# Moving the end of an FFT convolution between engines: residuals, layer statistics and weight splitting off the vector engine

## The chip, the cores and the metric

The kernel runs on one core of a Trainium2 chip. The core has a matrix engine (TensorE, PE), a vector engine (VectorE, DVE), an activation engine (ScalarE, ACT), a general engine (GpSimd, POOL) and a queue engine that mostly issues DMAs (SyncE, SP). Each runs its own instructions in order; they wait for one another by semaphores. PE writes its results to PSUM, from which DVE and ACT read them; everything else lies in SBUF. The metric is the time of one execution on the device in microseconds (us), smaller is better.

## The reference, cut to what matters

Four layers stand behind one another over a stream x of 2048 tokens by 640 features, each on the layer-normalized stream and each added to it:

```python
x = A_u
x = x + conv(layernorm(x))      # "a"
x = x + attention(layernorm(x)) # "b"
x = x + conv(layernorm(x))      # "c"
x = x + attention(layernorm(x)) # "d"

def conv(u):       # a state-space kernel K, 2048 taps for each feature
    y = irfft(rfft(u, 4096) * rfft(K, 4096))[:2048]
    return y + u * Dskip
def attention(x):  # 32 query heads of 20, one shared key and value head
    q, k, v = x @ wq, x @ wk, x @ wv
    return softmax(q k^T / sqrt(20)) v @ wo
```

Both convolutions have the same parameters, and so have both attentions. `layernorm` takes mean and variance over the 640 features of a token.

## The kernel before, in words

The stream stays in SBUF as `self.x`, [128 partitions, 16, 640]: 16 rows of 128 tokens, here called tokens tau = 0 to 15.

**A convolution** (`conv_layer`, line 664) goes over five chunks of 128 features (`NCH` = 5, `DC` = 128). For one chunk: ACT normalizes the 16 token rows (line 686); PE multiplies them with a table of cosines and sines (`dense`, line 570; `raw`, line 541, for the first chunk) and ACT copies the results out; DVE does the butterflies of a radix-8 transform (`fft8` with sign -1, fourteen calls, lines 95 and 98), the complex product with the spectrum of the kernel (`product`, eight calls, line 704) and the inverse butterflies (`fft8` with sign +1); PE multiplies by the inverse table (`inverse`, line 723), in four groups g of four token rows; and `residual` (line 730) adds a group to x on DVE. The spectrum A has 16 slots: token row tau needs slots 2t and 2t+1 with t = tau mod 8. The butterflies leave t = 0 and 4 first, then 2 and 6, and the odd t from the four scalar_tensor_tensor calls at the end. A group is tau = 4g to 4g+3, so the first group already needs odd t.

The order of PE, ACT and DVE is written out by hand (`manual_schedule`, line 671). `weave(calls, between)` puts other work between the calls of a list: (5, f) means that f is issued ahead of call 5. The residuals ("turns") of chunk c stand between the forward butterflies of chunk c+1 (turns 0 and 1) and its product (turns 2 and 3); turns 0 and 1 also issue the inverse of groups 2 and 3. Results of `inverse` alternate between two PSUM banks (`ps1`), so that groups 2 and 3 need the banks of 0 and 1 back.

In the last two chunks `residual` also takes statistics for the next layer normalization on DVE (`stats_part`): BATCH_NORM_STATS2 of a token row's first 512 features behind chunk 3 (line 600), of the last 128 behind chunk 4 (line 602), then their union (line 603). `norm_part(g)` turns them into scale and shift for a group (lines 624 to 631, with one square root on ACT). The loop over the last chunk's turns and `norm_part` (line 780) stands outside the hand-written order; there a planner with costs of its own orders the instructions of all engines. The same holds for the beginning of the attention.

**The attention's weights** are split in two parts whose sum is the fp32 value: `wh`, rounded to the matmul's format by ACT (line 795), and the rest `wl`, by DVE (line 798). `attn_weights` (line 800) loads them in six pieces (keys and values, then five of 128 rows of `wq`), one staging buffer `wst` for all, and the pieces are woven into the last chunk's product. This is done in both convolutions.

**The attention's beginning** (`_attn`, line 840): `prepare(nb)` normalizes four token rows on ACT (line 872), PE transposes them (line 881), ACT and DVE split them; `project` multiplies (line 898). The main loop behind it has the exponentials on ACT (line 1028) and products on PE (lines 1024 and 1038). `add` (line 1081) adds the attention's output to x.

Of the kernel before, what the change touches and what calls it, by code (L numbers as in the profile page):

```python
# [11 lines left out]
F32 = mybir.dt.float32  # L12
# [3 lines left out]
AF = mybir.ActivationFunctionType  # L16
# [14 lines left out]
EPS = 1e-5  # L31
SCALE = 20.0**-0.5
# [52 lines left out]
def fft8(nc, A, B, R, sg):  # L85

    ADD, SUB = ALU.add, ALU.subtract  # L90
    plus, minus = (ADD, SUB) if sg < 0 else (SUB, ADD)
    calls = []

    def tt(*a):
        calls.append(lambda: nc.vector.tensor_tensor(*a))  # L95

    def stt(*a):
        calls.append(lambda: nc.vector.scalar_tensor_tensor(*a, op0=ALU.mult, op1=ADD))
# [24 lines left out]
    return calls  # L123
# [12 lines left out]
class Net:  # L136
    def __init__(self, tc, ins):
        self.tc = tc
        self.nc = tc.nc
        self.ins = ins  # L140
        self.wfs = []
        self.sts = {}
        self.bank = 0

    def setup(self, ctx):
        tc, nc = self.tc, self.nc
        self.cp = ctx.enter_context(tc.tile_pool(name="cp", bufs=1))
        self.dr = ctx.enter_context(tc.tile_pool(name="dr", bufs=1, space=DRAM))
        self.ident = self.cp.tile([P, P], F32, name="ident")
        self.halfpi = self.cp.tile([P, 1], F32, name="halfpi")  # L150
        nc.vector.memset(self.halfpi, 0.5 * math.pi)
        self.xp = ctx.enter_context(tc.tile_pool(name="xp", bufs=1))
        self.x = self.xp.tile([P, 16, D], F32, name="x")
        self.mv = self.xp.tile([P, 16, 2], F32, name="mv")
        self.kd = self.dr.tile([NCH, P, 16 * DC], F32, name="kd")
        self.kh = self.dr.tile([NCH, P, 32 * DC], F32, name="kh")
# [438 lines left out]
    def stats_part(self, t, last):  # L595

        nc = self.nc
        if not last:
            self.sts[t] = self.xp.tile([P, 2, 6], F32, tag=f"st{t}", bufs=1, name=f"sp{t}")
            nc.vector.bn_stats(self.sts[t][:, 0], self.x[:, t, 0 : D - DC])  # L600
        else:
            nc.vector.bn_stats(self.sts[t][:, 1], self.x[:, t, D - DC : D])
            nc.vector.bn_aggr(self.mv[:, t], self.sts.pop(t).rearrange("p a b -> p (a b)"))
# [5 lines left out]
    def norm_part(self, g):  # L609
        ts = slice(4 * g, 4 * g + 4)  # L610
        self.rstd(self.xp, self.mv[:, ts], self.rs[:, ts], self.nmr[:, ts], 4)
# [7 lines left out]
    def rstd(self, pool, mv, out, nmr, n):  # L619

        nc = self.nc
        ve = pool.tile([P, n], F32, tag="ve", bufs=2, name="ve")
        sq = pool.tile([P, n], F32, tag="sq", bufs=2, name="sq")
        nc.vector.tensor_scalar(ve, mv[:, :, 1], EPS, None, ALU.add)
        nc.scalar.activation(sq, ve, AF.Sqrt)
        nc.vector.reciprocal(out, sq)
        nc.vector.tensor_tensor(sq, out, out, ALU.mult)
        nc.vector.tensor_tensor(sq, sq, ve, ALU.mult)
        nc.vector.tensor_scalar(sq, sq, -0.5, 1.5, ALU.mult, ALU.add)
        nc.vector.tensor_tensor(out, out, sq, ALU.mult)  # L630
        nc.vector.scalar_tensor_tensor(nmr, mv[:, :, 0], -1.0, out, op0=ALU.mult, op1=ALU.mult)
# [32 lines left out]
    def conv_layer(self, nm, first):  # L664
# [6 lines left out]
        with tc.manual_schedule(engines={mybir.EngineType.PE, mybir.EngineType.Activation,  # L671
# [41 lines left out]

            def inverse(c, g, A):
                y = self.ps1(f"y{nm}{c}{g}")
                v = A.rearrange("p s (k d) -> p s k d", k=2)
                for s in range(4):
                    tau = 4 * g + s
                    t, j = tau % 8, tau // 8
                    i = 0  # L720
                    for kk in range(2):
                        for c_ in range(2):
                            nc.tensor.matmul(y[:, s * DC : (s + 1) * DC], self.wi[:, t, j, c_, kk],  # L723
                                             v[:, 2 * t + c_, kk], start=(i == 0), stop=(i == 3))
                            i += 1
                return y

            def residual(c, g, y):
                xs = self.x[:, 4 * g : 4 * g + 4, c * DC : (c + 1) * DC]
                tt(xs, y.rearrange("p (t d) -> p t d", t=4), xs, ALU.add)  # L730
# [19 lines left out]
            pieces = []  # L750
            late = []
            for c in range(NCH):
                A = As.pop(c)
                mul = product(A, khs.pop(c)) + fft8(nc, A, B, R, +1)
                if c == NCH - 1:
                    late += zip((0, 1, 3, 5, 7, 11), pieces)
# [20 lines left out]
                if c + 2 == NCH - 1:  # L777
                    self.wfs.pop().close()
                    pieces = self.attn_weights()
# [6 lines left out]
    def attn_setup(self):  # L786
# [3 lines left out]
        self.mxd = dr.tile([33, 2, L], F32, name="mxd")  # L790

# [8 lines left out]
    def attn_weights(self):  # L800
# [6 lines left out]
        wl = wp.tile([P, 5, 692], F32R, name="wl")  # L807
        kv = wp.tile([P, 5, 52], F32, name="kv")
# [3 lines left out]
        self.wqs = stack, wh, wl  # L812

        def piece(k):
            wst = wp.tile([P, D], F32, tag="wst", bufs=1, name=f"wst{k}")
            nc.sync.dma_start(wst, ins["B_wq"][P * k : P * k + P])
            self.split(wh[:, k, 0:D], wl[:, k, 0:D], wst, act=True)

        return [lambda: self.split(wh[:, :, D:692], wl[:, :, D:692], kv, act=True)] + [
            lambda k=k: piece(k) for k in range(5)]  # L820
# [19 lines left out]
    def _attn(self, ctx, nm, out):  # L840
# [17 lines left out]
        with tc.tile_pool(name=f"pj{nm}", bufs=1, reuse_waits="tile") as pj:  # L858
# [7 lines left out]
            def prepare(nb):  # L866

                xs = []
                for i in range(4):
                    t = 4 * nb + i  # L870
                    x = pj.tile([P, D], F32, tag="x", bufs=4, name=f"x{nb}{i}")
                    nc.scalar.activation(x, self.x[:, t], AF.Identity, scale=self.rs[:, t : t + 1],
# [114 lines left out]
    def main_loop(self, ap, mp, kt, vt, nm, out):  # L987
# [93 lines left out]
        def add(nb, u, py, last):  # L1081

            i, half = u // 2, u % 2
            t = 4 * nb + i
# [142 lines left out]
```

## Time and profile before

| | |
|---|---|
| time, median of 3 runs | 3106.16 us (3105.56 to 3109.65) |
| span of the profiled execution, first to last instruction | 3104.8 us |
| busy in the span: PE, DVE, ACT | 2851.3, 1431.9, 2391.6 us |
| mean granted clock of PE | 0.977 |
| last two chunks of convolution "a" | about 567 to 683 us |
| last two chunks of convolution "c" | about 1909 to 2024 us |

The profile is that of one execution. The page of the profile says nothing of that execution's time but the span, which is 1.36 us below the median of the runs. In the timeline a row is a group of like instructions: start, length from the first start to the last end, engine, line, operation, output<-inputs with shapes, and count; in brackets stand the idle time of the engine before it and what ended it. A row that starts ahead of the end of the row before overlaps with it in the engine's pipeline; the distance of two starts is what an instruction costs its engine. In the windows a row is a stretch of time: its length, busy time with number of instructions, the granted clock of PE, and the share and rate of the DMA.

### The profile page before, as it was taken

To read this page: it belongs to the slowest core of one execution; us is meant where nothing else is said; L and a number is where in the kernel's file an instruction comes from. 1 tells how busy PE (TensorE), PEld (TensorE's weight loads), DVE (VectorE), ACT (ScalarE), POOL (GpSimd) and SP (SyncE) were. 2 spreads that over 40 slices of the span, in tenths; PEclk is the share of its full clock that TensorE was granted. 3 is DMA by queue.
4 is the path that set the end of the run, shared out by engine and by line. 5 is a ranking of instruction groups with operands and counts; after the bars stand their busy time and mean duration, and the time that the engine had idled before them with its cause. 6 is when DMAs were issued, how large, how long until landed. Compare 5 with 4: busy or idle time off the path is not lost. (4 is left out here: it accounts for less than half of the span.)

```text
span 3104.8 us, 52109 instructions
## 1 busy us (share of the span) xinstructions
PE 2851.3 (92%) x21638; PEld 1352.4 (44%) x21638; DVE 1431.9 (46%) x1853; ACT 2391.6 (77%) x2773; POOL 35.6 (1%) x102
## 2 busy tenths in 40 slices
PE   2888998949899999999999889498999999999999
PEld 0555888847323333323233489464223323233333
DVE  7888799973122232332222399931222222222223
ACT  5777343224799999999999633055999999999997
POOL 0000000000000000000000000000000000000000
PEclk9999999979899999999999999799999999999999
DMA  6011451114310000100100210132000100100100
GB/s 142 18 28 27 165 217 55 33 30 131 115 26 23 24 25 21 27 25 21 27 24 23 111 55 28 26 109 90 22 26 22 42 24 21 44 24 21 44 18 22
DMA packets 73630, 153.45 MB, mean 49 GB/s; under 512 B 22836, under 2 KB 28980, under 8 KB 69764
## 3 DMA queue, kind: packets, MB, share of 16 engines
q1 hardware_dynamic: 67336, 132.36, 14.5%
q0 software_dynamic: 4080, 16.67, 1.4%
q8 instruction: 174, 2.85, 0.4%
q10 hardware_dynamic: 1968, 0.98, 0.1%
q14 instruction: 72, 0.59, 0.1%
HBM read 93.42 MB, written 44.50 MB: 44 GB/s over the span
## 5 line engine op out<-in xcount | busy, mean ns | idle before, releaser
L1028 ACT ACTIVATE pt<-scb 128x1024 f32<-128x1024 f32 x1024 | 942.2, 1117 | 7.6 <-PE scb L1024 6.2
L1028 ACT ACTIVATE pt<-scd 128x1024 f32<-128x1024 f32 x1024 | 942.1, 1118 | 5.1 <-DMA qpd<-mxd 3.0
L1038 PE MATMUL pob<-pt,vt 128*32 128x512 f32 x4096 | 546.6, 606 | 4.5 <-DVE on L1055 3.5
L1038 PE MATMUL pod<-pt,vt 128*32 128x512 f32 x4096 | 546.4, 605 | 4.5 <-DVE on L1055 2.5
L1024 PE MATMUL scb<-qpb,kt 62*128 62x512 f32 x2048 | 385.5, 451 | 7.2 <-DVEq L977 6.9
L1024 PE MATMUL scd<-qpd,kt 62*128 62x512 f32 x2048 | 385.5, 451 | 4.8 <-DVEq L977 4.6
L1024 PEld LDWEIGHTS scb<-qpb,kt 62*128 62x128 f32 x2048 | 166.1, 185 | 402.7 <-ACT pt L1028 392.2
L1024 PEld LDWEIGHTS scd<-qpd,kt 62*128 62x128 f32 x2048 | 166.0, 185 | 400.4 <-ACT pt L1028 392.1
L1086 DVE TENSOR_TENSOR x<-pyd,x 128x320 f32<-128x320 f32 x146 | 71.8, 492 | 560.6 <-PE pyd L1098 560.6
L1086 DVE TENSOR_TENSOR x<-pyb,x 128x320 f32<-128x320 f32 x146 | 71.8, 492 | 547.4 <-PE pyb L1098 547.4
L1058 DVE RECIPROCAL rc<-rc 128x512 f32<-128x512 f32 x62 | 207.9, 3353 | 2.1
L1038 PEld LDWEIGHTS pob<-pt,vt 128*32 128x32 f32 x4096 | 80.7, 108 | 177.7 <-issue 159.6
L1038 PEld LDWEIGHTS pod<-pt,vt 128*32 128x32 f32 x4096 | 80.6, 108 | 177.6 <-issue 159.5
L415 PE MATMUL pk<-s,m 128*64 128x32 f32 x1280 | 130.7, 295 | 13.3 <-DVE s L406 13.3
L415 PE MATMUL pk<-c,e1r 128*64 128x32 f32 x1280 | 132.1, 297 | 11.4 <-DVE c L405 11.2
L415 PEld LDWEIGHTS pk<-c,e1r 128*64 128x64 f32 x1280 | 105.2, 221 | 79.6 <-issue 52.2
L723 PE MATMUL ya<-Aa,wi 128*128 128x128 f32 x640 | 78.6, 287 | 49.8 <-DVE Aa L95 46.7
L723 PE MATMUL yc<-Ac,wi 128*128 128x128 f32 x640 | 78.5, 286 | 46.8 <-DVE Ac L95 43.7
L570 PE MATMUL za<-xna,wf 128*128 128x256 f32 x512 | 113.2, 383 | 2.7 <-ACT xna L686 2.7
L415 PEld LDWEIGHTS pk<-s,m 128*64 128x64 f32 x1280 | 108.1, 226 | 15.9 <-DVE s L406 15.9
L570 PE MATMUL zc<-xnc,wf 128*128 128x256 f32 x512 | 111.5, 379 | 2.7 <-ACT xnc L686 2.7
L572 ACT ACTIVATE Aa<-za 128x1024 f32<-128x1024 f32 x16 | 16.4, 1024 | 118.4 <-PE za L570 116.8
(278 smaller groups left out, 3168.8 us busy)
## 6 DMA issues: line engine op xcount, KB each, us to landing
kh<-kh SPq DMA_DIRECT2D x10, 2048.0 KB
kh<-kn SPq DMA_DIRECT2D x5, 2048.0 KB
qhd<-qh SPq DMA_DIRECT2D x40, 256.0 KB
qld<-ql SPq DMA_DIRECT2D x40, 256.0 KB
qpb<-qhd SPq DMA_DIRECT2D x256, 40.0 KB
qpd<-qhd SPq DMA_DIRECT2D x256, 40.0 KB
ot<-on SPq DMA_DIRECT2D x216, 40.0 KB
wf<-in_c_wf POOLq DMA_DIRECT2D x16, 512.0 KB, 8.4
```

Of the source, the lines that this page charges most:

```text
L415: nc.tensor.matmul(PK[u][64 * par : 64 * par + 64, 32 * d : 32 * d + 32], e[u][:, d, par], c[u][:, d, par], start=first, stop=not first)
L570: nc.tensor.matmul(zv[:, :, c, kk], self.wf[:, t + 4 * h, j, c, kk], x, start=(n == 0), stop=(n == 3))
L572: nc.scalar.activation(A.rearrange("p (o s) d -> p o s d", o=2)[:, :, 2 * t : 2 * t + 2], z.rearrange("p (c o e) -> p o c e", c=2, o=2), A ...
L723: nc.tensor.matmul(y[:, s * DC : (s + 1) * DC], self.wi[:, t, j, c_, kk], v[:, 2 * t + c_, kk], start=(i == 0), stop=(i == 3))
L1024: nc.tensor.matmul(sc[:, 512 * par : 512 * par + 512], kt[rows, 128 * t : 128 * t + 128], qps[nb, hg, pr][rows], start=True, stop=True)
L1028: nc.scalar.activation(pt, sc, AF.Exp, scale=SCALE)
L1038: nc.tensor.matmul(po[32 * j : 32 * j + 32], vt[:, t], pts[step, j // 2][:, 512 * (j % 2) : 512 * (j % 2) + 512], start=(t == 0), stop=(t ...
L1058: nc.vector.reciprocal(rc, rc)
L1086: nc.vector.tensor_tensor(xh, py, xh, ALU.add)
```

## The change

It touches the two convolutions' last two chunks, and renames the order of token rows everywhere.

- **Order of token rows.** Groups become the rows `TAUS`: group 0 has tau 0, 4, 8, 12, group 1 has 2, 6, 10, 14, group 2 and 3 the odd ones. The attention goes over the rows in the same order.
- **Order of the butterflies.** In `fft8` the calls for t = 0 and 4 are calls 4 and 5, for t = 2 and 6 calls 8 and 9.
- **Stream on PE.** For chunks 3 and 4 `inverse` first multiplies the identity with x into the PSUM bank, and the transform is accumulated on it. `residual` for chunk 3 is then a copy to x on ACT; for chunk 4 it is part of the statistics.
- **Statistics on ACT.** `stats_first(g)`: for four token rows the sum over 512 features (a copy with `accum_out`), the negative mean, and the sum of squares about it. `stats_last(g, y)`: for the last 128 features a copy from PSUM to x with its sum, and the squares about the same shift. Two DVE instructions for all 16 rows (`stats_base`) and eleven small ones a group (`norm_part`) join them.
- **Weights.** The low part is taken on PE: identity times the weights minus identity times the high part, in PSUM, copied out by ACT. This is done in convolution "a" only, which stores both parts to DRAM (`whd`, `wld`, 1.77 MB each); convolution "c" loads them.
- The pieces of weights, `stats_first` and `stats_base` are woven into the last chunk's calls by a list.

```diff
+NA = D - DC
+FIRST = (0, 2, 1, 3)
+TAUS = [s + 4 * n for s in FIRST for n in range(4)]
...
     tt(B[:, 4:8], A[:, 0:4], A[:, 4:8], SUB)
-    tt(R[:, 0:2], A[:, 10:15:4], A[:, 11:16:4], ADD)
-    if sg < 0:
-        tt(R[:, 2:4], A[:, 11:16:4], A[:, 10:15:4], SUB)
-        tt(B[:, 12:16:3], R[:, 0:3:2], R[:, 3:0:-2], ADD)
-        tt(B[:, 14:12:-1], R[:, 0:3:2], R[:, 3:0:-2], SUB)
-    else:
-        tt(R[:, 2:4], A[:, 10:15:4], A[:, 11:16:4], SUB)
-        tt(B[:, 12:16:3], R[:, 2::-2], R[:, 1:4:2], SUB)
-        tt(B[:, 14:12:-1], R[:, 2::-2], R[:, 1:4:2], ADD)
     tt(B[:, 8:12:3], A[:, 8:10], A[:, 13:11:-1], plus)
     tt(B[:, 10:8:-1], A[:, 8:10], A[:, 13:11:-1], minus)
     tt(A[:, 0:2], B[:, 0:2], B[:, 2:4], ADD)
     tt(A[:, 8:10], B[:, 0:2], B[:, 2:4], SUB)
+    tt(R[:, 0:2], A[:, 10:15:4], A[:, 11:16:4], ADD)
+    if sg < 0:
+        tt(R[:, 2:4], A[:, 11:16:4], A[:, 10:15:4], SUB)
+    else:
+        tt(R[:, 2:4], A[:, 10:15:4], A[:, 11:16:4], SUB)
     tt(A[:, 4:14:9], B[:, 4:6], B[:, 7:5:-1], plus)
     tt(A[:, 12:4:-7], B[:, 4:6], B[:, 7:5:-1], minus)
+    if sg < 0:
+        tt(B[:, 12:16:3], R[:, 0:3:2], R[:, 3:0:-2], ADD)
+        tt(B[:, 14:12:-1], R[:, 0:3:2], R[:, 3:0:-2], SUB)
+    else:
+        tt(B[:, 12:16:3], R[:, 2::-2], R[:, 1:4:2], SUB)
+        tt(B[:, 14:12:-1], R[:, 2::-2], R[:, 1:4:2], ADD)
...
+    def stats_first(self, g, dump):
+        nc, sm = self.nc, self.sm
+        ps = range(4 * g, 4 * g + 4)
+        for p in ps:
+            nc.scalar.activation(dump(p), self.x[:, TAUS[p], 0:NA], AF.Copy, accum_out=sm["sum"][:, p : p + 1])
+        gs = slice(4 * g, 4 * g + 4)
+        nc.scalar.activation(sm["shift"][:, gs], sm["sum"][:, gs], AF.Copy, scale=-1.0 / NA)
+        for p in ps:
+            nc.scalar.activation(dump(p), self.x[:, TAUS[p], 0:NA], AF.Square, bias=sm["shift"][:, p : p + 1],
+                                 accum_out=sm["sq"][:, p : p + 1])
+    def stats_base(self):
+        nc, sm = self.nc, self.sm
+        nc.vector.tensor_scalar(sm["base"], sm["sq"], 1.0 / D, EPS, ALU.mult, ALU.add)
+        nc.vector.tensor_scalar(sm["part"], sm["shift"], DC / D, None, ALU.mult)
+    def stats_last(self, g, y, dump):
+        nc, sm = self.nc, self.sm
+        for n in range(4):
+            p = 4 * g + n
+            nc.scalar.activation(self.x[:, TAUS[p], NA:D], y[:, DC * n : DC * n + DC], AF.Copy,
+                                 accum_out=sm["sumb"][:, p : p + 1])
+        for n in range(4):
+            p = 4 * g + n
+            nc.scalar.activation(dump(n)[:, 0:DC], y[:, DC * n : DC * n + DC], AF.Square,
+                                 bias=sm["shift"][:, p : p + 1], accum_out=sm["sqb"][:, p : p + 1])
...
             def inverse(c, g, A):
+                whole = c >= NCH - 2
+                if whole:
+                    nc.tensor.matmul(y, self.ident, stream(c, g), start=True, stop=False)
...
             def residual(c, g, y):
-                xs = self.x[:, 4 * g : 4 * g + 4, c * DC : (c + 1) * DC]
-                tt(xs, y.rearrange("p (t d) -> p t d", t=4), xs, ALU.add)
-                for tau in range(4 * g, 4 * g + 4):
-                    if c >= NCH - 2:
-                        self.stats_part(tau, c == NCH - 1)
+                if c < NCH - 2:
+                    tt(stream(c, g), y.rearrange("p (t d) -> p t d", t=4), stream(c, g), ALU.add)
+                elif c == NCH - 2:
+                    nc.scalar.activation(stream(c, g), y.rearrange("p (t d) -> p t d", t=4), AF.Copy)
+                else:
+                    self.stats_last(g, y, dump)
...
                 if c == NCH - 1:
-                    late += zip((0, 1, 3, 5, 7, 11), pieces)
+                    first_, second = self.attn_weights(scr, nm == "a")
+                    late = ([(0, late[0][1]), (0, first_[0]), (1, late[1][1]), (1, first_[1])]
+                            + [(1, lambda g=g: self.stats_first(g, dump)) for g in (0,)]
+                            + [(2, second[0]), (2, first_[2]), (2, lambda: self.stats_first(1, dump)),
+                               (3, second[1]), (3, first_[3]), (3, lambda: self.stats_first(2, dump)),
+                               (4, second[2]), (4, first_[4]), (4, lambda: self.stats_first(3, dump)),
+                               (5, second[3]), (5, first_[5]), (6, second[4]), (6, second[5]),
+                               (12, self.stats_base)])
                 weave(mul, late)
...
+        if not fresh:
+            for w, dst in parts:
+                nc.sync.dma_start(w, dst.rearrange("p (k n) -> p k n", k=5))
+            return [lambda: None] * 6, [lambda: None] * 6
...
+        def first(k):
...
+            nc.scalar.activation(hi, src, AF.Copy)
+            for o, a, _ in cuts:
+                nc.tensor.matmul(o, self.ident, a, start=True, stop=False)
+            for o, _, b in cuts:
+                nc.tensor.matmul(o, self.minus, b.bitcast(F32), start=False, stop=True)
+        def second(k):
...
+            nc.scalar.activation(ends(k)[1], src, AF.Copy)
+            if k == 5:
+                for w, dst in parts:
+                    nc.sync.dma_start(dst.rearrange("p (k n) -> p k n", k=5), w)
```

More of the change, by code (lines that the diff above doesn't have):

```diff
@@ L151, in setup @@
         nc.vector.memset(self.halfpi, 0.5 * math.pi)
+        self.minus = self.cp.tile([P, P], F32, name="minus")
         self.xp = ctx.enter_context(tc.tile_pool(name="xp", bufs=1))
@@ L154, in setup @@
         self.mv = self.xp.tile([P, 16, 2], F32, name="mv")
+        self.sm = {n: self.xp.tile([P, 16], F32, name=f"sm{n}")
+                   for n in ("sum", "shift", "sq", "sumb", "sqb", "base", "part")}
         self.kd = self.dr.tile([NCH, P, 16 * DC], F32, name="kd")
@@ L624, in rstd @@
         nc.vector.tensor_scalar(ve, mv[:, :, 1], EPS, None, ALU.add)
[L625 to L630, printed above, removed]
+        self.root(ve, sq, out)
         nc.vector.scalar_tensor_tensor(nmr, mv[:, :, 0], -1.0, out, op0=ALU.mult, op1=ALU.mult)
@@ L723, in inverse @@
                             nc.tensor.matmul(y[:, s * DC : (s + 1) * DC], self.wi[:, t, j, c_, kk],
-                                             v[:, 2 * t + c_, kk], start=(i == 0), stop=(i == 3))
+                                             v[:, 2 * t + c_, kk], start=(i == 0 and not whole),
+                                             stop=(i == 3 and (s == 3 or not whole)))
                             i += 1
@@ L790, in attn_setup @@
         self.mxd = dr.tile([33, 2, L], F32, name="mxd")
+        self.whd = dr.tile([P, 5 * 692], F32, name="whd")
+        self.wld = dr.tile([P, 5 * 692], F32, name="wld")
+        self.nc.scalar.activation(self.minus, self.ident, AF.Copy, scale=-1.0)
     def split(self, hi, lo, src, act=False):
@@ L1083, in add @@
             i, half = u // 2, u % 2
-            t = 4 * nb + i
+            t = TAUS[4 * nb + i]
             xh = self.x[:, t, 320 * half : 320 * half + 320]
```

67 lines of the change are left out of this document (44 added, 23 removed).

## The prediction, made before the result

> **What bounds the kernel now.** The span of the profiled execution is 3104.8 us; the three timed runs have a median of 3106.16, 1.36 more. The page gives no other time of that execution, so I take savings from the span and subtract them from the median.
>
> I first read the timeline of VectorE (DVE) over the end of the first convolution. Columns: start, length of the group, engine, line, operation, count, and in brackets the idle time before it.
>
> ```profile
> 579.18 2.29 DVE L704 TENSOR_TENSOR B<-Aa,kh 128x2048 f32<-128x2048 f32 x1
> ...
> 581.39 0.68 DVE L730 TENSOR_TENSOR x<-ya,x 128x512 f32<-128x512 f32 x1
> 581.99 2.28 DVE L704 TENSOR_TENSOR R<-Aa,kh 128x2048 f32<-128x2048 f32 x1
> ...
> 598.36 2.36 DVE L95 TENSOR_TENSOR B<-Aa 128x1024 f32<-128x1024 f32 x2
> 600.64 1.29 DVE L95 TENSOR_TENSOR R<-Aa 128x512 f32<-128x512 f32 x2
> ...
> 609.19 2.35 DVE L95 TENSOR_TENSOR B<-Aa 128x1024 f32<-128x1024 f32 x2
> ...
> 613.39 0.68 DVE L730 TENSOR_TENSOR x<-ya,x 128x512 f32<-128x512 f32 x1
> 614.11 2.47 DVE L600 BATCH_NORM_STATS2 sp<-x 128x6 f32<-128x512 f32 x4
> 616.50 0.67 DVE L95 TENSOR_TENSOR B<-R 128x512 f32<-128x512 f32 x1
> ...
> 626.20 0.42 DVE L798 TENSOR_TENSOR wl<-kv,wh 128x260 fp32r<-128x260 f32 x1
> 626.54 2.29 DVE L704 TENSOR_TENSOR B<-Aa,kh 128x2048 f32<-128x2048 f32 x1
> ...
> 631.85 0.81 DVE L798 TENSOR_TENSOR wl<-wst,wh 128x640 fp32r<-128x640 f32 x1
> 632.58 2.28 DVE L704 TENSOR_TENSOR R<-Aa,kh 128x2048 f32<-128x2048 f32 x1
> ...
> 662.68 2.49 DVE L98 SCALAR_TENSOR_TENSOR Aa<-B 128x512 f32<-128x512 f32 x4
> 668.59 0.69 DVE L730 TENSOR_TENSOR x<-ya,x 128x512 f32<-128x512 f32 x1 [3.42 <-PE ya L723]
> ```
>
> No row has idle time until 668.59, so DVE sets the pace up to the last butterfly, which ends at 665.17. Then TensorE (PE), by its timeline:
>
> ```profile
> 579.87 27.79 PE L570 MATMUL za<-xna,wf 128*128 128x256 f32 x128
> 607.49 10.88 PE L723 MATMUL ya<-Aa,wi 128*128 128x128 f32 x96
> 620.83 3.84 PE L723 MATMUL ya<-Aa,wi 128*128 128x128 f32 x32 [2.46 <-DVE x L730]
> 661.11 2.05 PE L723 MATMUL ya<-Aa,wi 128*128 128x128 f32 x8 [36.43 <-DVE Aa L95]
> 663.51 15.76 PE L723 MATMUL ya<-Aa,wi 128*128 128x128 f32 x120 [0.36 <-DVE Aa L98]
> 680.28 0.55 PE L881 MATMUL ptb<-ident,x 128*128 128x128 f32 x3 [1.01 <-ACT x L872]
> ```
>
> PE waits 36.43 us for DVE, then its last inverse transforms end at 679.27, 14.1 us behind the butterfly, and the attention's first tokens wait for that end. The second convolution has the same rows 1341.6 us later (its butterfly group starts at 2004.41, and 2010.18 stands for 668.59); I give its times less 1341.6.
>
> ```profile
> 2004.41 2.48 DVE L98 SCALAR_TENSOR_TENSOR Ac<-B 128x512 f32<-128x512 f32 x4
> 2010.18 0.69 DVE L730 TENSOR_TENSOR x<-yc,x 128x512 f32<-128x512 f32 x1 [3.28 <-PE yc L723]
> ```
>
> So the path is DVE to 665.17, PE to 679.27, then ScalarE (ACT) at line 872.
>
> **What leaves DVE.** In the last stretch four residuals of the chunk before the last, with their statistics, take 616.50 - 613.39 = 3.11 us each, 12.4 in all. Five low parts of the weights take 632.58 - 631.85 = 0.73 each, with the small one of keys and values (626.54 - 626.20 = 0.34) 4.0. Together 16.4 us. Without them: forward butterflies from 609.19 in 609.19 - 598.36 = 10.83; product 598.36 - 579.18 less two residuals of 0.6 (581.39 to 581.99), 18.0, ends at 638.0; four calls of the inverse butterflies (2.28 and two of 0.6), 3.5. At **641.5** DVE reaches call 12, where the change puts stats_base. The reordered butterflies cost the same: the stall in the pair at 600.64 (1.32 from start to start where two calls take 1.20) goes, and one like it comes before the first scalar_tensor_tensor, whose input is then written just ahead.
>
> **What comes to ACT.** stats_base needs the squares of all sixteen tokens, and these are 32 passes of 512 elements on ACT. Rows for their price, from the timeline of ACT:
>
> ```profile
> 681.76 0.19 ACT L625 ACTIVATE sq<-ve 128x4 f32<-128x4 f32 x1
> 681.86 0.90 ACT L872 ACTIVATE x<-x,nmrna,rsna 128x640 f32<-128x640 f32 x1
> ...
> 705.28 0.59 ACT L911 ACTIVATE qs<-pqb 128x512 fp32r<-128x512 f32 x1
> ...
> 469.39 0.87 ACT L686 ACTIVATE xna<-x,nmra,rsa 128x128 f32<-128x128 f32 x2
> 470.16 0.48 ACT L686 ACTIVATE xna<-x,nmrma,rsma 128x128 f32<-128x128 f32 x1
> ```
>
> A pass of 512 lasts 0.59; neighbours overlap by about 0.1 (0.19 long, next start 0.10 later), so 0.50 from start to start. 128 elements with a scale and a bias from memory: 0.77 for two, 0.385 each; from 512 to 128 without operands I estimate 0.20, so about 0.09 an operand. A Square with a bias takes 0.59. What no row shows is the sum along the row (accum_out). I treat it as one more small instruction for each pass: between nothing (it rides along; below that it can't go, since a second output shortens no pass) and 0.19 (the small row's whole length). I take that row's pitch, **0.10**, because ACT's neighbours overlap in every row here. A group of four tokens: 4 x 0.60 + 4 x 0.69 + 0.3 for the shift and two waits on it = 5.5; four groups 21.8.
>
> They can't start early. In ACT's order they stand behind the fourth residual copy, and that needs all of PE's inverse transforms of the chunk: 10.88 / 3 = 3.63 a group, plus the added identity product (512 columns in two instructions; the 256-column row gives 27.79 / 128 = 0.217, doubled 0.43, 0.87 in all; no row has this shape, and the bounds 0.43 and 1.3 would move each convolution by up to 7 x 0.43 = 3). 607.49 + 4 x 4.5 = 625.5, copy and hand-over 0.6: 626.1. In the second convolution stats_first ends at 626.1 + 21.8 + 0.2 = **648.1**: DVE waits 6.6 us at call 12 and passes the wait on, for every later call is queued behind. In the first, ACT also has four high parts (640 wide, 0.63) and three low parts between (two of 0.63, one of 0.3), less one high part that follows: 4.1 more, **652.2**.
>
> **The new tail.** After stats_base (two calls, 0.3) two butterfly calls (1.2) release group 0: 1.65 with the hand-over, where PE formerly waited for nearly all. PE's old tail took 679.27 - 661.11 - 0.36 = 17.8; three identity products not hidden add 2.6. Second convolution: 648.1 + 1.65 + 20.4 = 670.2, **9.1 earlier** than 679.27. In the first, PE must before that take the minus-product of the last weights (their high part leaves ACT at 652.2 + 1.4): 640 columns, then the identity, 2.0 at full clock. Is the clock full? Windows of PE, with the granted clock behind the busy time:
>
> ```profile
> 626.50:627.00 0.50, 0.00 (x0) 1.00 0.00 0
> 627.00:627.50 0.50, 0.00 (x0) 0.50 0.00 0
> ...
> 667.00:668.00 1.00, 1.00 (x7) 0.52 0.12 37
> 668.00:669.00 1.00, 1.00 (x11) 1.00 0.00 0
> ...
> 468.00:469.00 1.00, 0.43 (x3) 1.00 1.01 426
> ...
> 472.00:473.00 1.00, 0.00 (x0) 1.00 0.00 0
> 473.00:474.00 1.00, 0.00 (x0) 0.70 0.00 0
> ```
>
> After 36 us of idling the clock stays at half until 668.0, 6.9 us after the first matmul. With that, 6.9 + 15.6 of full-speed work + 1.4 = 23.9 behind 652.2: 676.1, **3.2 earlier** (6.7 if the weights' products have warmed it).
>
> ACT's part per group of the last chunk, four copies of 128 (0.20 + 0.10) and four squares (0.29 + 0.10), is 2.8, less than PE's 4.5, so it hides behind the next group, except for the last. That one I put ahead of the attention's tokens on ACT, for both wait for the same last matmul and it stands first in the program: **2.8 later** in each convolution. Formerly DVE did this beside ACT.
>
> So PE now pauses from its last inverse to the first transpose for 2.8 + 0.9 + 0.1 = 3.8 us instead of 1.01. The rows above show the clock falling 2.3 us after the last matmul (624.67 to 627.0), and in another place about 5 (468.4 to 473.7). 3.8 lies midway: I count one fall in two pauses. Its price is between 1.4 (the last eleven transposes at half rate) and 3.4 (half of 6.9): 2.4.
>
> TensorE: Matmul & The Clock Gate of the Trainium skill, section Part 1: The HAM clock gate (the "warmup" mystery), says the clock is halved after about 3.4 us idle and freed after about 3.4 us busy. Here the trace disagrees on the second (6.9) and straddles the first; by the rule both pauses would fall, the fourth rival below.
>
> **Costed at nothing.** The first convolution stores 3.5 MB of split weights on SP's queue; the stores wait for ACT's last low part at about 656, and behind them stand the loads for the attention, the mask ob first, which a projection uses some 30 us later. Without that cover each microsecond of lateness would count. The second loads the same bytes from about 608, 70 us ahead of need. PE's y banks are now released by ACT; with two of them and 2.8 against 4.5 us the release is early. Chunks 0 to 2 have the same work on both engines; the token order changes only addresses.
>
> **Sum.** 9.1 + 3.2 - 2 x 2.8 - 2.4 = 4.3 earlier: **3101.9**.
>
> **Rivals.**
> 1. *Sums cost a full instruction on ACT.* 0.19 instead of 0.10 over 40 sums in each of two convolutions is 7.2 later: 3109.1, slower than before. It decides from 0.10 + 4.3 / 80 = 0.154. For: the sum may have to wait for the pass to drain; against: the small row's pitch of 0.10.
> 2. *Sums ride along:* 80 x 0.10 = 8 earlier, 3093.9. For: no row shows a second instruction; against: the result must be written to its own place.
> 3. *The planner puts the tokens ahead of the last group on ACT* (this stretch is outside the hand-written order): 5.6 and the cold pause back, 3093.9. For: one of the second convolution's tokens runs before PE's last matmul already (2019.66 against 2020.96). Against: program order.
>
> ```profile
> 2019.66 0.91 ACT L872 ACTIVATE x<-x,nmrnc,rsnc 128x640 f32<-128x640 f32 x1
> 2020.96 1.73 ACT L872 ACTIVATE x<-x,nmrnc,rsnc 128x640 f32<-128x640 f32 x2 [0.39 <-PE yc L723]
> ```
>
> 4. *Both pauses halve the clock:* 2.4 more, 3104.3; neither: 3099.5.
> 5. *ACT keeps up, and DVE's 16.4 us are won whole:* PE would end near 641.5 + 22.1 in both, 15.7 earlier less 2.8: 3080. It needs 32 passes in 641.5 - 626.1 = 15.4, under 0.50 each: the rows speak against it.
>
> **How the numbers follow.** Forecast 0.38; rivals 1: 0.20, 2: 0.13, 3: 0.10, 4: 0.15 (0.08 of it with neither cold), 5: 0.04. A measurement of this kernel tells about 0.2%, 6.2 us, from no change. Faster than 3099.9: rivals 2, 3, 5, those 0.08 and a quarter of the forecast, 0.45. Slower than 3112.4 needs rival 1 beyond 0.19 or with both pauses cold, or a misplaced wait in the planned tail: 0.14. The same: 0.41. Range 3091 to 3111: rivals 1 to 4 with 2 us about them; rival 5 and the slower end stay out.
>
> **What would show it.** On DVE a wait of some 7 (second) and 11 us (first) on ACT at stats_base; without it rival 5 holds. On ACT the start-to-start time of the 512-wide passes: 0.60 and 0.69 by the forecast, 0.09 more by rival 1. Eight small passes between PE's last inverse and line 872's successor, or not (rival 3). The granted clock at the first transposes. PE's last inverse 9 and 3 us earlier. A DVE wait elsewhere in the last chunk, or PE waiting for weights in a projection, would make the prediction wrong.

## The result and the profile after

The changed kernel takes **3127.93 us** (3127.32 to 3128.39) where the kernel before takes 3107.45 (3105.56 to 3109.65): a ratio of 1.0068, with a 95% interval of 1.0056 to 1.0079. It is 20.5 us slower. The forecast was 3101.9 us, in a range of 3091 to 3111, and faster than before.

The page of the changed kernel gives the span and the engines' busy time first.

```profile
span 3125.5 us, 52436 instructions
PE 2883.2 (92%) x21714; PEld 1366.0 (44%) x21714; DVE 1388.9 (44%) x1765; ACT 2460.1 (79%) x3046; POOL 35.1 (1%) x101
```

DVE lost 43 us of work (1431.9 before) and ACT got 68.5 (2391.6 before). These sums were to be expected, and they say nothing of the 20 us. To find those, I followed one landmark after another through both timelines of DVE and PE. These are rows of the kernel before that the prediction did not show: the generation of the convolution kernel near its end (line 401, the last but one of its twenty rows), the forward butterflies of the last chunk of convolution c (line 95), and the first projection of each attention (line 898).

```profile
316.35 1.22 DVE L401 SCALAR_TENSOR_TENSOR m<-m,s 128x1024 f32<-128x1024 f32 x1
1950.91 2.35 DVE L95 TENSOR_TENSOR B<-Ac 128x1024 f32<-128x1024 f32 x2
685.95 0.44 PE L898 MATMUL pqb<-xh,wh 128*52 128x512 f32 x1 [1.72 <-DVE xl L798]
2027.33 0.43 PE L898 MATMUL pqd<-xh,wh 128*52 128x512 f32 x1 [1.72 <-DVE xl L798]
```

The same landmarks in the kernel after, from its timelines of DVE (line 408 is the old 401, line 98 the old 95):

```profile
346.01 1.22 DVE L408 SCALAR_TENSOR_TENSOR m<-m,s 128x1024 f32<-128x1024 f32 x1
637.78 2.35 DVE L98 TENSOR_TENSOR B<-Aa 128x1024 f32<-128x1024 f32 x2
1978.75 2.35 DVE L98 TENSOR_TENSOR B<-Ac 128x1024 f32<-128x1024 f32 x2
```

and of PE, with the end of convolution a and then that of c:

```profile
682.29 2.50 PE L899 MATMUL pw<-wh,minus 128*128 128x512 f32 x4 [2.98 <-ACT wh L895]
...
685.77 3.73 PE L770 MATMUL ya<-Aa,wi 128*128 128x128 f32 x32
...
699.06 3.73 PE L770 MATMUL ya<-Aa,wi 128*128 128x128 f32 x32
706.23 5.12 PE L970 MATMUL ptb<-ident,x 128*128 128x128 f32 x20 [3.43 <-ACT x L961]
712.45 0.67 PE L987 MATMUL pqb<-xh,wh 128*52 128x512 f32 x1 [1.09 <-DVE xl L860]
...
715.90 0.42 PE L987 MATMUL pqb<-xl,wh 128*52 128x512 f32 x1
...
2018.96 5.87 PE L770 MATMUL yc<-Ac,wi 128*128 128x128 f32 x32 [23.29 <-DVE Ac L98]
...
2041.56 5.12 PE L970 MATMUL ptd<-ident,x 128*128 128x128 f32 x20 [3.43 <-ACT x L961]
2047.78 0.43 PE L987 MATMUL pqd<-xh,wh 128*52 128x512 f32 x1 [1.09 <-DVE xl L860]
```

After less before, landmark by landmark:

| landmark | later by, us |
|---|---|
| kernel generation, last row but one (346.01 - 316.35) | 29.66 |
| convolution a, last chunk's forward butterflies (637.78 - 609.19) | 28.59 |
| first projection behind a (712.45 - 685.95) | 26.50 |
| convolution c, last chunk's forward butterflies (1978.75 - 1950.91) | 27.84 |
| first projection behind c (2047.78 - 2027.33) | 20.45 |
| end of the span (3125.5 - 3104.8) | 20.7 |

So the stretch that the diff is about got faster: a's end by 2.1 us up to the first projection (1.3 of it are lost again right behind), c's end by 7.4. And about 30 us were lost before, where the diff seems to do nothing: line 401's first row stands at 66.28 us before and at 95.92 after, so they are lost by then already. The waits of the kernel after, over its first 120 us, name the place (engine, line and tile, what it waited for, us in total, times, longest):

```profile
ACT minus L852 <- DMA ident<-in_c_id: 32.7, 1, 32.7
...
DVE e1r L404 <- ACT m L394: 27.8, 1, 27.8
```

Line 852 is the copy that makes the negative identity matrix (`self.minus`, ident times -1), which the low parts of the weights first need at 654 us. It is one small instruction of 0.31 us. On the timeline of ACT it stands here:

```profile
49.99 1.15 ACT L378 ACTIVATE c<-fa,halfpi 128x1024 f32<-128x1024 f32 x1
83.87 0.31 ACT L852 ACTIVATE minus<-ident 128x128 f32<-128x128 f32 x1 [32.73 <-DMA ident<-in_c_id]
84.08 1.04 ACT L376 ACTIVATE fa<-f 128x1024 f32<-128x1024 f32 x1
```

between the cosine of the generation's first unit (line 378) and the absolute value for the second (line 376). And the queue of SP tells why it waits, first after, then before:

```profile
75.98 1.84 SPq L219 DMA_DIRECT2D tm<-hlw  x3
...
78.50 0.58 SPq L502 DMA_DIRECT2D ident<-in_c_id  x1
```

```profile
78.48 0.59 SPq L495 DMA_DIRECT2D ident<-in_c_id  x1
```

The load of ident was nearly the last of SP's initial queue in the kernel before too, behind dozens of loads that take the queue some 0.6 us each (1.84 for three in the first row). Nobody needed ident early, so the late load cost nothing. The copy does need it, and it stands in `attn_setup`, outside the order written by hand: its place in ACT's queue was the planner's choice, and the planner put it behind the first unit's cosine. ACT works in order, so everything behind it waited 32.7 us, and DVE waited 27.8 us for ACT's `m`.

My theory, then: this one copy costs some 28 to 30 us, and the rest of the change is worth about 8 to 9. The rival: the 30 us belong to something else that the change does early (a different plan of the generation's work, longer code), and the wait at `minus` only happens to cover it.

### The profile page after: what moved, and what is told of

Same layout as the page of the kernel before. It is cut to its first block, busy times and chain, and to the rows that moved or that the text cites. A ratio compares the mean times of both kernels' runs of the same rounds, so it can differ in the third digit from the quotient of the medians.

```text
span 3125.5 us, 52436 instructions
## 1 busy us (share of the span) xinstructions
PE 2883.2 (92%) x21714; PEld 1366.0 (44%) x21714; DVE 1388.9 (44%) x1765; ACT 2460.1 (79%) x3046; POOL 35.1 (1%) x101
## 5 line engine op out<-in xcount | busy, mean ns | idle before, releaser
L579 ACT ACTIVATE Ac<-zc 128x1024 f32<-128x1024 f32 x16 | 16.4, 1024 | 113.7 <-PE zc L577 113.7
```

The lines of the kernel that those rows point to most:

```text
L579: nc.scalar.activation(A.rearrange("p (o s) d -> p o s d", o=2)[:, :, 2 * t : 2 * t + 2], z.rearrange("p (c o e) -> p o c e", c=2, o=2), A ...
```

## The experiments

**The copy alone.** Three kernels tell the two apart: the changed kernel without the early copy, the kernel before with nothing but the copy (its result is not used), and the changed kernel with the copy left to the planner as it was, but its operand loaded early.

```diff
 # e1_minus_late, against the changed kernel
     def attn_setup(self):
...
-        self.nc.scalar.activation(self.minus, self.ident, AF.Copy, scale=-1.0)
...
     def attn_weights(self, scr, fresh):
         if not fresh:
             ...
+        nc.scalar.activation(self.minus, self.ident, AF.Copy, scale=-1.0)
 # e2_before_plus_minus, against the kernel before
+        self.minus = self.cp.tile([P, P], F32, name="minus")
...
     def attn_setup(self):
...
+        self.nc.scalar.activation(self.minus, self.ident, AF.Copy, scale=-1.0)
 # e3_ident_early, against the changed kernel: the load moved from the end
 # of SP's initial loads (line 502) to the second place (line 320)
+            nc.sync.dma_start(self.ident, ins["c_id"])
...
-                    nc.sync.dma_start(self.ident, ins["c_id"])
```

> The changed kernel with one edit: the copy that makes the negative identity is issued in the hand-written order at the start of the last chunk of the first convolution, instead of ahead of the convolution, outside that order. Theory A (ACT's queue stood 32.7 us behind this copy, which waited for the identity's load at the end of SP's queue, while the convolution kernel was generated): 28 to 30 us faster than the changed kernel, 3098 to 3100 us, and the generation ends at about 316 us as before the change. Theory B (the 29.7 us come from the new tiles' places or the order of the loads): about 3128 us. Theory C (the convolutions' ends lost the time): about 3128 us with the generation on time.

> The kernel before with this one part of the change added: the negative identity's tile and the copy that makes it, at the same place in the program; nothing uses it. Theory A: 28 to 30 us slower than before, about 3136 us, with ACT waiting some 33 us for the identity's load. Theories B (a matter of the larger tiles or loads) and C: within 2 us of before, 3107 us.

> The changed kernel with the identity's load as the second of SP's queue instead of nearly its last; the copy stays outside the hand-written order. Theory A: nothing to wait for, so 28 to 30 us faster than the changed kernel, 3098 to 3100 us, up to 0.5 us more because one load goes ahead of the first inputs. Theory B: about 3128 us.

Measured beside a kernel before of 3108.05 us: e1 **3099.12** (ratio 0.9972, interval 0.9960 to 0.9983), e2 **3136.36** (1.0090, 1.0073 to 1.0107), e3 **3100.16** (0.9975, 0.9966 to 0.9985). The row of the copy on ACT's timeline, in e1, in e2 and in e3:

```profile
616.71 0.30 ACT L875 ACTIVATE minus<-ident 128x128 f32<-128x128 f32 x1
```

```profile
83.53 0.31 ACT L792 ACTIVATE minus<-ident 128x128 f32<-128x128 f32 x1 [32.69 <-DMA ident<-in_c_id]
```

```profile
4.65 0.31 ACT L852 ACTIVATE minus<-ident 128x128 f32<-128x128 f32 x1 [0.78 <-DMA ident<-in_c_id]
```

The same instruction of 0.3 us waits for nothing, 32.69 us, and 0.78 us. The generation's last row but one follows it: 317.19 us in e1, 345.70 in e2, 317.70 in e3. The kernel before pays 28.3 us for it without any other part of the change (3136.36 - 3108.05); the changed kernel gets 28.8 back without it (3127.93 - 3099.12). The rival falls, for the two agree. e3 shows that an early load is enough and that the copy need not be put into the order by hand; it does not show that the place in ACT's queue is indifferent, for with the early load the planner put the copy elsewhere, at 4.65 us, ahead of the generation. The rest of the change is a gain of 9 us, 0.3%.

**What still holds the convolutions' end.** DVE still waits 11 us (a) and 7 us (c) at `stats_base`, as the prediction had it (the rows stand below, by its steps), and all later butterflies are queued behind. e4 puts `stats_base` behind most of the butterflies; nobody needs it before the first `norm_part`.

```diff
 # e4_base_last, against e1
-                               (12, self.stats_base)])
+                               (22, self.stats_base)])
```

> As the first kernel of this set, and stats_base moved from call 12 to behind the last butterfly. In the changed kernel DVE waited 10.7 and 6.7 us at call 12 for ACT's sums. If those waits set PE's start (theory of the prediction): PE's inverse of group 0 starts earlier, but group 2 then needs its bank back from ACT, whose queue has the sums and the weights first; in the first convolution PE also has the last weights ahead of group 0. By hand 4 to 6 us in each convolution, so 8 to 12 us below the first kernel, 3087 to 3092 us. Rival: ACT's queue holds PE as long as DVE did, then about 3099 us, within 2 us of the first kernel.

Measured: **3091.47** us (ratio 0.9946, 0.9929 to 0.9963), 7.7 below e1, a little less than the 8 to 12 expected. On PE's timeline of e4, convolution a, then c:

```profile
654.59 2.07 PE L899 MATMUL pw<-wh,minus 128*128 128x512 f32 x4 [2.75 <-ACT wh L895]
...
658.15 3.89 PE L770 MATMUL ya<-Aa,wi 128*128 128x128 f32 x32
...
1982.35 5.69 PE L770 MATMUL yc<-Ac,wi 128*128 128x128 f32 x32 [16.35 <-DVE Ac L98]
```

In c, PE's first inverse group starts after a pause of 16.35 us instead of 23.29 (the row at 2018.96 of the changed kernel; e1 has the same): 6.9 of the 7.7 us. In a the group starts no earlier (657.49 us in e1). There it stands in PE's queue behind the last products of the weights, and these wait for a high part that ACT makes behind the sums. One wait gone, the next one is late at the same place.

**ACT's idle stretch, and its last group.** ACT works little from 602 to 627 us in convolution a, while PE does the fourth chunk's inverse. e5 issues the sums of the first two groups right behind the copies of their residuals, ahead of the weights, those of the third among the weights, and those of the last behind the last high part. For this the weights are also set up one chunk earlier. e6 instead takes the last group of the last chunk off ACT: DVE copies it to x and takes its whole statistics. e7 does both. e8 is e5 with the old order of the butterflies' calls.

```diff
 # e5_stats_early, against e4: woven into the last chunk
+                    late = [(0, t2), (0, first_[0]), (0, first_[1]), (1, t3), (1, second[0]), (1, first_[2]),
+                            (1, s2), (2, second[1]), (2, first_[3]), (3, second[2]), (3, first_[4]),
+                            (4, second[3]), (4, first_[5]), (4, s3), (5, second[4]), (5, second[5]),
+                            (99, self.stats_base)]
...
 # and in turn(g) of the fourth chunk
+                    if c == NCH - 2 and g < 2:
+                        self.stats_first(g, dump)
 # e6_last_group_vector, against e4, in residual() and at the end
+                else:
+                    nc.vector.tensor_copy(stream(c, g), y.rearrange("p (t d) -> p t d", t=4))
+                    for t in TAUS[12:]:
+                        self.stats(t)
...
-        self.norm_part(3)
+        self.rstd(self.xp, self.mv[:, FIRST[3] : 16 : 4], self.rs[:, 12:16], self.nmr[:, 12:16], 4)
```

> The version with the negative identity late and the base of the statistics moved back (3091.5 us), with the squares and sums of a group issued right behind that group's fourth-chunk residual, two of the four groups of them ahead of the weights' splitting, and the splitting ahead of the last one. Theory: in convolution a TensorE's first inverse group of the last chunk stood 14 us late (658.15 us against the 643.8 us at which its butterflies are ready) only because ScalarE held the weights' last high parts behind the sums; with the sums in ScalarE's idle stretch of 602 to 627 us the group starts at about 644 to 646, and the time is 3077 to 3081 us. Convolution c has no such wait and gains nothing. Rival (ScalarE is simply too busy there: 22 us of sums and 8 us of splitting from 613 us on are all needed before the group): the group starts at about 650 or later, 3083 to 3090 us.

> The version of 3091.5 us, with the last group's last chunk copied and its statistics taken whole on VectorE, which is idle there. Theory: ScalarE's 2.4 us of copies, squares and reads for that group stand ahead of attention's first tokens, and TensorE pauses 3.4 us for them; without them the transposes start about 2.5 to 3.4 us earlier in each convolution, and the clock no longer falls in convolution a: 3083 to 3087 us. Rival (VectorE's statistics then stand ahead of the split of the transposed tokens, some 4 to 5 us): nothing gained, 3090 to 3093 us.

> Both of these edits. If both theories hold and do not overlap: 3069 to 3074 us. If only the earlier sums help: 3077 to 3081; if neither: 3090 to 3093.

> The version with the sums early, with the butterflies' calls back in the order of the kernel before. The two calls that the first inverse group needs are then ninth and tenth instead of fifth and sixth, four calls of 0.6 us later. If TensorE's inverse is what ends the convolutions once the sums no longer hold it, its first group starts 2.4 us later in each of the two convolutions, and the time is 4 to 5 us above the version with the new order. If VectorE or ScalarE still ends them, no difference.

Measured beside a kernel before of 3107.76 us: e5 **3078.46** (ratio 0.9908, 0.9892 to 0.9925), e6 **3087.84** (0.9936, 0.9920 to 0.9953), e7 **3073.67** (0.9890, 0.9873 to 0.9906), e8 **3088.28** (0.9939, 0.9922 to 0.9955).

e5 on PE's timeline, end of convolution a:

```profile
643.05 3.84 PE L770 MATMUL ya<-Aa,wi 128*128 128x128 f32 x32 [1.57 <-DVE Aa L98]
...
663.62 0.55 PE L972 MATMUL ptb<-ident,x 128*128 128x128 f32 x3 [3.43 <-ACT x L963]
...
669.83 0.44 PE L989 MATMUL pqb<-xh,wh 128*52 128x512 f32 x1 [1.36 <-DVE xl L861]
```

The group starts at 643.05, as soon as its butterflies are done, 15 us before e4's 658.15. ACT had the room; what held the group was the order of its queue (in e4 ACT waits for no load in this stretch, so the earlier set-up of the weights is not the cause). In e6 the transposes behind a start so:

```profile
675.87 0.55 PE L974 MATMUL ptb<-ident,x 128*128 128x128 f32 x3 [1.01 <-ACT x L965]
```

The pause ahead of them is 1.01 us instead of 3.43, and e6 gains 3.6 us on e4, 0.8 less than the least I expected; e7 gains 4.8 on e5, at the upper end of its range. e5's theory holds. e6's holds for the pause, but not for the clock: it was to stay up in a, and it falls a little later. From 682.58 to 685.99 us it is at half, and the projections from the fifth to the twelfth start 0.43 us apart, where in e4 all start 0.23 apart. That gives back 1.6 us of the gain in a.

e8 lost more than I expected of it: 9.8 us instead of 4 to 5. Its timeline of PE, end of convolution a:

```profile
645.53 6.26 PE L768 MATMUL ya<-Aa,wi 128*128 128x128 f32 x32 [3.98 <-DVE Aa L98]
...
674.73 0.67 PE L987 MATMUL pqb<-xh,wh 128*52 128x512 f32 x1 [1.09 <-DVE xl L859]
```

The group starts 2.5 us later than in e5, as expected. But the pause ahead of it is now 3.98 us instead of 1.57, and its 32 matmuls take 6.26 us instead of 3.84: another 2.4. And the first projection is 0.67 us long instead of 0.44. In c the group starts behind a pause of 18.56 us instead of 16.15 and takes 6.27 instead of 5.81. And in both convolutions the first seven projections run at half clock, where e5 has none that do: another 1.4 us each. Together that is 10.6 us between the two profiled executions. So a late start costs a second time, through TensorE's clock. The new order of the calls is worth 9.8 us in the kernel of e5, where nothing else holds the group.

**The clock.** In e7 the pause ahead of the first group is 2.10 us in a and 16.69 in c, and the group takes 5.46 and 5.65 us. e9 fills these pauses with products of the identity that are thrown away, 2 in a and 18 in c; e10 is e7 again beside it.

```diff
 # e9_pe_kept_busy, against e7, in inverse()
+                if c == NCH - 1 and g == 0:
+                    for _ in range(2 if nm == "a" else 18):
+                        nc.tensor.matmul(y, self.ident, stream(c, g), start=True, stop=True)
```

> The version with both edits, with products of the identity that are thrown away in TensorE's pause ahead of the last chunk's first inverse group: 2 in convolution a (pause 2.10 us), 18 in convolution c (pause 16.69 us, 18 at 0.86 us are 15.5). Theory: the first group's 32 matmuls take 5.46 and 5.65 us instead of 3.73 because the pause let the clock fall to half; kept busy, both take 3.7 to 3.8, and the time falls by 3.0 to 3.7 us below the version with both edits. Rival 1 (the first group waits for its operands from VectorE, not for the clock): no change. Rival 2 (the extra work draws the clock down later): the group is faster and the time is the same or longer.

> The version with both edits once more, as the measure beside it: 3072 to 3075 us.

Measured beside a kernel before of 3108.21 us: e9 **3072.89** (3072.07 to 3074.51; ratio 0.9889, 0.9871 to 0.9906), e10 **3073.63** (3072.90 to 3074.42; 0.9889, 0.9871 to 0.9907). The difference of 0.7 us lies within the two spreads. First e10, PE's timeline at the end of a:

```profile
643.50 5.47 PE L770 MATMUL ya<-Aa,wi 128*128 128x128 f32 x32 [2.10 <-DVE Aa L98]
...
669.01 0.43 PE L993 MATMUL pqb<-xh,wh 128*52 128x512 f32 x1 [1.88 <-DVE xl L865]
```

and two windows, one inside that group and one over the transposes behind it. A row has the stretch, its length, busy time and count of PE, PEld, DVE, ACT and POOL, then the granted clock and the DMA:

```profile
644.11:647.52 3.41, 3.41 (x18) 3.41 (x18) 3.41 (x6) 1.17 (x2) 0.00 (x0) 0.50 0.46 195
...
664.59:668.00 3.41, 2.01 (x15) 1.49 (x14) 2.93 (x14) 2.65 (x5) 0.00 (x0) 1.00 0.00 0
```

Then e9, PE's timeline, and behind a's rows the first group of c:

```profile
642.39 3.84 PE L773 MATMUL ya<-Aa,wi 128*128 128x128 f32 x32 [0.39 <-DVE Aa L98]
...
666.67 0.67 PE L996 MATMUL pqb<-xh,wh 128*52 128x512 f32 x1 [1.09 <-DVE xl L868]
...
669.27 0.45 PE L996 MATMUL pqb<-xh,wh 128*52 128x512 f32 x1
...
1966.43 3.84 PE L773 MATMUL yc<-Ac,wi 128*128 128x128 f32 x32 [1.24 <-DVE Ac L98]
```

and windows of e9 over a's transposes:

```profile
659.14:662.55 3.41, 1.87 (x13) 1.12 (x11) 3.28 (x11) 2.99 (x4) 0.00 (x0) 1.00 0.00 0
662.55:665.97 3.42, 2.78 (x13) 2.21 (x11) 2.63 (x13) 2.16 (x4) 0.00 (x0) 0.50 0.00 0
```

The theory is right in its first half: kept busy, the group takes 3.84 us in both convolutions, 1.6 and 1.8 less. But rival 2 is right about the time. The clock now falls later. In a it does so at the small pauses around the transposes, and the first six projections start 0.43 us apart (666.67 to 669.27 is 2.60 us) instead of the 0.23 of full clock; in c it falls at the first projection (1990.34), and the first eight start 0.43 apart. What the group gains, the transposes and projections give back.

Why do the pauses around a's transposes halve the clock in e9, when the same pauses leave it full in e10? The traces show a reason: in each of them the granted clock changes only on a grid with steps of 3.41 us. In e10 the changes near the end of a are at 644.11 and 647.52, in e9 at 662.55 and 669.38, two steps apart. The clock of a step goes by how busy PE was in the step before. A step at full clock in which PE was busy for less than 0.43 of the time was followed by half clock in every trace of this case, one with more than 0.55 never, and between these both occur. In e9 the pauses fall into one step (659.14 to 662.55, PE busy for 1.87 us, 0.55 of it), and the clock falls. In e10 they spread over two (661.17 to 664.59 with 0.63, 664.59 to 668.00 with 0.59), and it stays. The pauses ahead of the first group fit too: the step around them has 0.38 in e10 and falls, 0.54 in e5 and stays. Where the grid lies against the kernel's start differs from trace to trace, so which pause costs a fall is partly luck. Only one execution of each kernel is profiled, so how often e9 loses what it won is not shown; its four runs range over 2.4 us.

## Why the prediction was wrong

**The step that failed** is the list "Costed at nothing". It went through the stores, the loads, the banks and the order of tokens, and left out one added instruction, the copy that makes the negative identity. Its price by itself, 0.3 us, is indeed nothing; but it is issued in `attn_setup`, where the planner chooses its place, and its operand's load was nearly the last of SP's first queue. Both could be read before: the load's row in the queue of SP (78.48 us), and that `attn_setup` stands outside the order written by hand. Where the planner would put the copy could not be read. Of the rivals only the first made the kernel slower than before, and it looked for the loss in the convolutions' end; a misplaced wait was thought of, but in the planned tail and not in the first 100 us. e1 and e2 price the missing term at 28.8 and 28.3 us, and with the early load of e3 27.8 of it are gone. Forecast and missing term make 3101.9 + 28.5 = 3130.4, 2.5 above the result. The forecast was taken from a time before of 3106.16, and beside the result it was 3107.45; from there it is 3131.7, 3.7 above.

The other steps, held against the kernel after (its times less 28.59 in a, less 27.84 in c, to stand on the clock of before):

- **What leaves DVE: right.** DVE reaches `stats_base` at 681.06 - 10.68 - 28.59 = 641.8, forecast 641.5. Its waits there:

```profile
681.06 0.17 DVE L616 TENSOR_SCALAR smbase<-smsq 128x16 f32<-128x16 f32 x1 [10.68 <-ACT xnas L611]
...
2018.07 0.17 DVE L616 TENSOR_SCALAR smbase<-smsq 128x16 f32<-128x16 f32 x1 [6.71 <-ACT xncs L611]
```

The forecast was 11 us in a and 7 in c; the sums end at 652.5 in a (forecast 652.2).

- **The sum's price on ACT: right, rivals 1, 2 and 5 fell.** A pass with a sum is two instructions on the timeline of ACT:

```profile
655.01 0.62 ACT L607 ACTIVATE xnas<-x 128x512 f32<-128x512 f32 x1
655.53 0.19 ACT L607 ACTIVATION_READ_ACCUMULATOR xnas<-x 128x1 f32 x1
655.62 0.62 ACT L607 ACTIVATE xnas<-x 128x512 f32<-128x512 f32 x1
...
657.83 0.72 ACT L611 ACTIVATE xnas<-x,smshift 128x512 f32<-128x512 f32 x1
...
658.55 0.71 ACT L611 ACTIVATE xnas<-x,smshift 128x512 f32<-128x512 f32 x1
```

The read lasts 0.19 and is followed after 0.09: the pitch that the prediction took from the small row (0.10), not its length. A copy with its sum is 0.61 from start to start (forecast 0.60), a square 0.70 to 0.72 (0.69).

- **The new tail: right in kind, too dear by 1.5 to 2 us.** PE's last inverse ends at 702.79 in a, 5.1 earlier on the clock of before (forecast 3.2), and at 2041.56 - 3.43 = 2038.13 in c, 10.6 earlier (9.1). In a the row at 685.77 shows the reason: the first group takes 3.73 us, full speed, so the weights' products had already brought the clock back, the case that the prediction had at 6.7. They paid for it: the last four take 2.50 us where four at full clock take 1.25, and from their start to the group's are 3.48 us (685.77 - 682.29) where the prediction had 2.0. In c the first group took 5.87, 2.1 more than a warm one, where the prediction carried the 6.9 us of half clock over from the old tail.

- **The last group on ACT: right in kind, 2.4 instead of 2.8**, and ahead of the tokens; rival 3 fell. The pause is 3.43 us (forecast 3.8).

- **One of two pauses halves the clock: wrong in the count, and near in the total by luck.** Windows of the kernel after, the pause of a and then that of c:

```profile
703.00:705.00 2.00, 0.00 (x0) 0.00 (x0) 0.40 (x3) 2.00 (x15) 0.00 (x0) 1.00 0.00 0
705.00:706.00 1.00, 0.00 (x0) 0.00 (x0) 0.32 (x2) 1.00 (x4) 0.00 (x0) 0.85 0.00 0
...
715.00:716.00 1.00, 1.00 (x4) 0.51 (x3) 0.00 (x0) 0.92 (x2) 0.00 (x0) 0.53 0.00 0
716.00:717.00 1.00, 1.00 (x6) 0.56 (x5) 0.00 (x0) 0.00 (x0) 0.00 (x0) 1.00 0.00 0
```

```profile
2040.00:2041.00 1.00, 0.00 (x0) 0.00 (x0) 0.23 (x2) 1.00 (x6) 0.00 (x0) 0.66 0.00 0
```

The clock fell in both, rival 4. But in c it was full again at the first projection (2047.78, 0.43 us long), and in a it came back only at 716, after eight projections in 3.45 us (712.45 to 715.90), 0.43 each against 0.23 at full clock. The transposes hide most of a fall: from their start to the first projection is 6.22 us in both, 5.67 before in a and 5.74 in e10, both at full clock. So a fall cost 0.55 under the transposes and 8 x 0.2 = 1.6 under a's projections: 2.7 in all, where the forecast had 2.4. That is two falls of 2.15 and 0.55 in place of one of 2.4. The fall that the prediction read at 473.7 lies at 473.4, for its row from 473 to 474 has 0.70.

Together: 1.9 and 1.5 us from the tails, 2 x 0.4 from the last groups, less 0.3 for the clock, 3.9 better than the forecast's 4.3, so 8.2. The change without the early copy (e1) measured 8.9 (3108.05 - 3099.12), so 0.7 us stays unexplained.

## What to carry to other kernels

Every added instruction has three prices: its time, its place in an in-order queue, and when its last operand arrives. Where a planner chooses the place, look up the operand's load in the DMA queue before you put the instruction down as free; a load that nobody missed for 80 us becomes a stall for the whole queue. And where an edit speeds up the stretch that it aims at and the total gets worse, lay both timelines side by side from the beginning, landmark by landmark, before you look at the stretch itself.

## What the runs showed of the hardware

- A sum along the row costs ACT a separate instruction of 0.19 us that takes 0.09 of its queue.
- The granted clock changed only on a grid with steps of 3.41 us, which lies differently against the kernel in each trace. A step at full clock with PE busy for less than 0.43 of the time was always followed by half clock, one with more than 0.55 never. So a fall can come late: in the kernel after it came 2.9 us behind PE's last inverse (702.79 to 705.71).
- Pauses of 2.10 and 3.98 us ahead of the first inverse group cost it 1.6 and 2.4 us (e10, e8), one of 1.57 us nothing (e5). TensorE: Matmul & The Clock Gate of the Trainium skill, section Part 1: The HAM clock gate (the "warmup" mystery), has the clock halved after about 3.4 us without work and freed after about 3.4 us of sustained work. Here the length agrees, but a step need not be empty: in e10 the one with the pause of 2.10 us was busy for 0.38 and the clock fell. In dense work it came back after one step (644.11 to 647.52 in e10); among transposes with small gaps it took three in the kernel after (705.71 to 715.95), the first two with PE busy for 0.85 and 0.68.
- Work that keeps the clock up in one pause can leave the fall to a later one (e9): 1.6 and 1.8 us won in the inverse, about as much lost in the transposes and projections.
